# Windowed attention with 20-wide heads: 64 score products in the edge set become 32, and 16 in each main set become 24

## The chip, the core and the metric

The kernel runs on one NeuronCore of a Trainium2 chip, in one launch. The metric is the device time of one execution in microseconds (us). Its engines work side by side, each through an instruction list of its own, and wait for each other by semaphores: PE (TensorE, matrix products; its weight loads are shown apart as PEld), ACT (ScalarE), DVE (VectorE), POOL (GpSimd) and SP, which here only issues transfers (DMA). Products leave PE into PSUM, a memory of eight banks; from there ACT or DVE take them into SBUF.

## What is computed

A transformer block over a sequence of 2048 rows of 640 values, with 32 heads of 20 values and a causal window of 256 keys:

```python
mod = (silu(c) @ w_mod)                    # six vectors: sa, ca, ga, sb, cb, gb
h = layernorm(x) * (1 + ca) + sa
q, k, v = split(h @ wqkv)                  # 32 heads of 20
s = q @ k.T * 20 ** -0.5
mask = (i - j >= 0) & (i - j < 256)
o = softmax(where(mask, s, -1e9)) @ v
x = x + ga * (o @ wo)
h = layernorm(x) * (1 + cb) + sb
x = x + gb * ((sigmoid(h @ w_gate) * (h @ w_up)) @ w_down)
```

w_gate and w_up are 640x1536, w_down is 1536x640. Everything is bf16 outside PSUM.

## The kernel before

The sequence is cut into 8 chunks of 256 rows (two blocks of 128). For each chunk `a` the kernel does `ln1` (layer norm), `qkv` (three projections; Q and K are brought into the layout "head values on partitions" by transposing transfers), `attention`, `outproj` and `mlp`. Work of several chunks is under way at a time, so that PE always has dense products (128x128 weights, L684) to do between the steps of the attention.

Four heads `j` lie on partitions 0, 32, 64 and 96, so a head's product uses 20 rows of one 32-row strip of PE's array, and four heads can run in the array at once. Eight groups of four heads make 32 heads. `attention(a)` treats the groups in two halves `q` of four groups `k`. For chunks 1 to 7 each half consists of five score sets, then one burst:

- The edge set (`edge_set`, L1000) takes the corners of the band for all four groups: 64 products, each of 64 keys by 64 queries, with the array cut into strips of 32 rows and 64 columns (eight places; `tp=(32 * j, 64 * half)`). ACT turns its 2048 columns of PSUM into exponentials in the tile G (L1022).
- Four main sets (`main_set`, L1028), one for each `k`: 16 products of 128 keys, with the array cut into strips of 32 rows and all 128 columns (four places), 192, 64, 64 and 192 queries wide (`PIECES`, L1026). ACT writes the exponentials into a tile E, in eight stretches of 256 out of every 384 columns (L1048). POOL then clears what lies outside the band by four selections of 512 columns (L1057): two in place, two that read the corners from G and write them into the free ends of E.
- The burst (`burst`) multiplies the exponentials by V: 64 products for each half, four 32-column strips of the array at once, a row of ones in V giving the softmax sum. DVE transposes and divides the result (`norm`), and `close` sends it through DRAM by transfers into the layout that `outproj` needs.

PSUM has one score buffer (`p_S`, four banks), so a set's products can start only after ACT has read the set before. The other four banks (`p_M`) serve everything else. E has five buffers of 3072 columns (`NE`, `EW`), G one of 2048.

A burst is done together with a score set of the next half: with `AFTER = 1` it stands in PE's list just ahead of the second of the five sets (`with_pv`). Before the change the sets of a half come in the order edge, 0, 1, 2, 3 (`plan`), so a half's burst follows the next half's edge set.

The order of every engine is fixed. Each step is an operation (`Prog.op`) with an estimated length; the list `PLAN` names, in one sequence, the operation and its engine, and `schedule` and `emit` only walk it: they give buffers, and put a wait on each operation for what it depends on. Nothing is decided at run time, so an engine whose next instruction waits stands still. Transfers are issued by SP and by ACT (`XE`, `OUTE`); which of them, and which engine does a copy or a scaling that several could do, is also in `PLAN`. At the start ten transfers bring c, the first rows of x, half of wq and five pieces of w_mod; the five products of w_mod with silu(c) (`fnA`) give the vectors `mA`, without which the first projection can't start.

## Time and profile before

| | |
|---|---|
| time, median of 3 runs | 327.04 us (326.96 to 327.34) |
| span of the profiled execution, first to last instruction | 324.6 us |
| PE busy | 318.6 us, 5044 products recorded |
| POOL busy | 187.1 us, of it 141.2 us in the masks of L1057 |
| ACT busy | 212.5 us, of it 131.3 us in the exponentials of L1048 and L1022 |
| DVE busy | 205.6 us |

The profile of an execution gives its span; its time with what lies around the span is not recorded apart, and the median of the runs is 2.4 us above the span. PE's weight loads run beside its products. A product's record has its start as the engine saw it and an end that is modelled, about 0.2 us later, so products overlap; what a group of products costs is read from start to start, which is what the chain of waits shows. In the chain, "PE S L685" is a score set, "PE M L685" a burst, "PE M L684" dense products.

### The profile page before, as it was taken

To read this page: it belongs to the slowest core of one execution; us is meant where nothing else is said; L and a number is where in the kernel's file an instruction comes from. 1 tells how busy PE (TensorE), PEld (TensorE's weight loads), DVE (VectorE), ACT (ScalarE), POOL (GpSimd) and SP (SyncE) were. 2 spreads that over 40 slices of the span, in tenths; PEclk is the share of its full clock that TensorE was granted. 3 is DMA by queue.
4 is the path that set the end of the run, shared out by engine and by line. 5 is a ranking of instruction groups with operands and counts; after the bars stand their busy time and mean duration, and the time that the engine had idled before them with its cause. 6 is when DMAs were issued, how large, how long until landed. Compare 5 with 4: busy or idle time off the path is not lost.

```text
span 324.6 us, 11948 instructions
## 1 busy us (share of the span) xinstructions
PE 318.6 (98%) x5044; PEld 239.1 (74%) x5045; DVE 205.6 (63%) x421; ACT 212.5 (65%) x228; POOL 187.1 (58%) x326
## 2 busy tenths in 40 slices
...
PEclk9999999999999999999999999999999999999999
...
GB/s 248 370 379 182 304 182 214 208 201 313 111 107 39 152 79 99 92 98 117 57 75 60 95 26 22 103 91 95 8 58 99 46 63 63 50 55 41 63 0 42
DMA packets 73023, 38.20 MB, mean 118 GB/s; under 512 B 46602, under 2 KB 71690, under 8 KB 72970
## 3 DMA queue, kind: packets, MB, share of 16 engines
...
## 4 chain that ended last, share of the span: by engine, by line
PE 91%; DMA 3%; SPq 1%; ACT 1%; issue 1%; DVE 1%; POOL 0%; POOLq 0%; DVEq 0%; ACTq 0%
PE M L684 75%; PE S L685 9%; PE M L685 6%; DMA wd<-in_w_mod_dram 2%; DMA h2T<-x 1%; SPq L574 1%; ACT E L1022 1%; SPq L808 1%; ACT hT L825 0%; DVE hT L826 0%; POOL E L1057 0%; POOL h2T L826 0%; PE S L684 0%; DVE x L801 0%; DVE V L901 0%
## 5 line engine op out<-in xcount | busy, mean ns | idle before, releaser
L1057 POOL TENSOR_SCALAR_AFFINE_SELECT E<-E 128x512 bf16<-128x512 bf16 x224 | 141.2, 662 | 65.8 <-PE S L685 25.5
L1048 ACT ACTIVATE E<-S 128x2048 bf16<-128x2048 f32 x56 | 105.0, 1876 | 32.9 <-PE S L685 32.5
L684 PE MATMUL M<-h2T,wu 128*128 128x256 bf16 x480 | 71.2, 273 | 0.1
L684 PE MATMUL M<-h2T,wg 128*128 128x256 bf16 x480 | 66.1, 273 | 0.0
L684 PE MATMUL M<-wd,hh 128*128 128x320 bf16 (+2 forms) x396 | 56.8, 295 | 0.0
L684 PEld LDWEIGHTS M<-h2T,wg 128*128 128x128 bf16 x480 | 46.3, 98 | 6.5
L684 PEld LDWEIGHTS M<-h2T,wu 128*128 128x128 bf16 x480 | 44.1, 98 | 9.1 <-issue 0.6
L1276 ACT ACTIVATE sig<-M 128x512 f32<-128x512 f32 x48 | 28.5, 595 | 33.8 <-PE M L684 32.0
L1278 DVE SCALAR_TENSOR_TENSOR hh<-sig,M 128x512 bf16<-128x512 f32 x48 | 32.2, 678 | 28.3 <-ACT sig L1276 20.7
L684 PEld LDWEIGHTS M<-wd,hh 128*128 128x128 bf16 x396 | 37.7, 98 | 13.8
L685 PE MATMUL S<-QT,KT 20*64 20x64 bf16 (+4 forms) x1856 | 35.0, 211 | 0.1
L685 PEld LDWEIGHTS S<-QT,KT 20*128 20x128 bf16 (+1 forms) x1856 | 22.1, 98 | 17.3 <-issue 8.5
L1022 ACT ACTIVATE E<-S 128x2048 bf16<-128x2048 f32 x14 | 26.3, 1877 | 13.1 <-PE S L685 12.7
L1297 DVE TENSOR_TENSOR x<-M,x 128x320 bf16<-128x320 f32 (+2 forms) x33 | 15.7, 480 | 30.2 <-PE M L684 29.9
L1142 DVE STREAM_TRANSPOSE T<-M 128x512 f32<-128x512 f32 x32 | 21.7, 699 | 13.8 <-PE S L685 12.8
L779 DVE BATCH_NORM_STATS2 st<-x 128x6 f32<-128x320 bf16 x64 | 28.6, 476 | 0.7 <-DMA x<-in_A_x_dram 0.3
L684 PE MATMUL M<-wv,hT 128*128 128x320 bf16 x160 | 27.4, 300 | 0.0
L684 PE MATMUL M<-wq,hT 128*128 128x320 bf16 x160 | 26.6, 300 | 0.4 <-issue 0.4
L684 PE MATMUL M<-wk,hT 128*128 128x320 bf16 x160 | 26.8, 299 | 0.0
L684 PE MATMUL M<-wo,oT 128*128 128x320 bf16 x160 | 25.5, 299 | 0.3 <-ACT hT L825 0.3
L1231 DVE TENSOR_TENSOR x<-M,x 128x320 bf16<-128x320 f32 x32 | 15.3, 489 | 13.0 <-PE M L684 12.8
L685 PE MATMUL M<-E,V 128*32 128x256 bf16 (+1 forms) x960 | 22.8, 246 | 0.1
...
## 6 DMA issues: line engine op xcount, KB each, us to landing
...
```

Source lines behind the costliest of these rows:

```text
L574: return e.dma_start(dst(), src())
L684: return e.matmul(o, l, r, start=st, stop=sp, skip_group_check=True)
L685: return e.matmul(o, l, r, start=st, stop=sp, tile_position=tp, skip_group_check=True)
L779: A("dve", lambda e, g, bi=bi, j=j: e.bn_stats(v(bi * 12 + j * 6, 6), src[bi].ap[:, j * 320:(j + 1) * 320]), 0.48, reads=[src[bi].r()], wr ...
L1022: A("act", lambda e, eng: e.activation(G.ap[:], Sp.ap[:], ACT.Exp, scale=SM_SCALE), 1.876, reads=[Sp.r()], writes=[G.r()], prio=3, tag=f"e ...
L1048: A("act", lambda e, eng: e.activation(wide()[:, :, 64:320], Sp.ap[:].rearrange("p j (t c) -> p (j t) c", c=256), ACT.Exp, scale=SM_SCALE) ...
L1057: A("pool", lambda e, eng, ap=ap, inp=inp, pat=pat, base=base, cm=cm: e.affine_select(ap(), inp(), pattern=pat, compare_op=ALU.is_ge, fill ...
L1142: A("dve", lambda e, g, h=h: e.transpose(T1.ap[:, 512 * h:512 * h + 512], X[h].ap), 0.694, reads=[X[h].r()], writes=[T1.r(h)], prio=3.5, t ...
L1231: A("dve", lambda e, g, ps=ps, bi=bi, half=half: e.tensor_tensor(x1[bi].ap[:, half * 320:half * 320 + 320], ps.ap[:, 0:320], x1[bi].ap[:, ...
L1276: A("act", lambda e, g, pg=pg, sg=sg: e.activation(sg.ap[:], pg.ap[:], ACT.Tanh, scale=0.5), c_act(512), reads=[pg.r()], writes=[sg.r()], ...
L1278: A("dve", lambda e, g, pu=pu, sg=sg, f0=f0: e.scalar_tensor_tensor(out=hh.ap[:, f0:f0 + 2, :], in0=sg.ap[:].rearrange("p (a b) -> p a b", ...
L1297: A("dve", lambda e, g, ps=ps, bi=bi, c0=c0, n=n: e.tensor_tensor(x1[bi].ap[:, c0:c0 + n], ps.ap[:, 0:n], x1[bi].ap[:, c0:c0 + n], op=ALU. ...
```

## The change

Per half, chunks 1 to 7:

- The edge set is replaced by `ends_set`: only the two outer pieces of the band (block -2 for the first 64 queries, block 1 for the last 64), as 32 products of 128 keys by 64 queries, four places at once. Its exponentials go to the outer quarters of a G that is twice as wide (4096 columns), and POOL clears two triangles in it by two selections of 1024 columns.
- Each main set has 24 products of 64 keys, in three pairs of 256, 192 and 64 queries: the halves of a key block lie beside each other in the array (eight places; `PIECES`). The set then holds the two inner key blocks in full plus two corners of 64x64 that were parked in columns which the band leaves empty. ACT writes 2048 columns in one piece into E, which has 2048 columns now and six buffers. POOL does, for each of two sides, a selection of 256 columns that carries a corner from E into the inner quarters of G (`side`), and then one of 512 columns in place (`mask`).
- The burst reads blocks 0 and -1 from E and blocks -2 and 1 from G. The number and the widths of its products stay.
- The order of the sets is 0, 1, ends, 2, 3. The burst of the half before still comes ahead of the second set, which is now a main set, and follows main set 0.
- `PLAN` is new as a whole: all engines' orders, and which engine does what. Against the kernel before, ACT has 14 more operations, 8 of them transfers that SP issued; DVE 11 fewer; POOL 33 more, 28 of them masks and sides; SP 8 fewer. PE has the same 959 operations. At the start, the second piece of wq is issued ahead of w_mod and the first x rows of SP come after the first piece of w_mod; DVE does both statistics of x before the last step of silu(c), on which the w_mod products wait.

In the diff the numbers of `PLAN` are left out, and the last lines, which only hand G on.

```diff
@@ -351,118 +351,120 @@
 
 
 PLAN = [
...
 ]
 TR1 = 2
 NPH = 2
@@ -486,8 +488,8 @@
 FILL = 1
 WSE = (("dve", "pool"), ("dve", "pool"))
 QMAX = 4.5
-NE = 5
-EW = 3072
+NE = 6
+EW = 2048
 PAIR = 0
 PAIRO = 0
 XHP = ((2, 0), (3, 0), (4, 0), (4, 1), (5, 0), (5, 1))
@@ -537,9 +539,9 @@
     p_QT = sbpool("QT", 3, [128, NG, CH])
     p_KT = sbpool("KT", 4, [128, NG, CH])
     p_V = sbpool("V", 8, [128, H * VW + 10])
-    Eall = sb("E", [128, NE * EW + 2048])
+    Eall = sb("E", [128, NE * EW + 4096])
     p_E = Pool("E", [Eall[:, i * EW:(i + 1) * EW] for i in range(NE)])
-    p_G = Pool("G", [Eall[:, NE * EW:NE * EW + 2048].rearrange("p (j c) -> p j c", j=4)])
+    p_G = Pool("G", [Eall[:, NE * EW:NE * EW + 4096]])
     p_T1 = sbpool("T1", 1, [128, 1024], F32)
     p_Tn = sbpool("Tn", 1, [128, 1024])
     p_On = sbpool("On", 1, [128, 1024])
@@ -981,7 +983,7 @@
         if a == 0:
             return [([(0, 0, 0, 2, 0), (1, 0, 0, 2, 2)], ((0, 2, 2),), ()), ([(2, 0, 0, 2, 0), (3, 0, 0, 2, 2)], ((0, 2, 2),), ()),
                     ([(k, 1, 1, 1, k) for k in range(4)], ((0, 1, 4),), ())]
-        return [None, 0, 1, 2, 3]
+        return [0, 1, None, 2, 3]
 
     def with_pv(name, sc, dur, rd, tiles, before, mode):
         if before is None:
@@ -997,33 +999,42 @@
         return A("pe", both_of, pd + 0.09 + dur, reads=list(rd), writes=[tiles[-1].r(), X[0].r(), X[1].r()], prio=10, lat=0.2,
                  tag=f"pvs{pa}", extra=last["s"], mode=2, mout=mode, hold=tiles[:-1] + X)
 
-    def edge_set(a, q, before):
-        G, Sp = Tile(p_G, f"G{a}_{q}"), Tile(p_S, f"S{a}_{q}e")
-
-        def sc(e, eng):
-            ins = None
-            for k in range(4):
-                gi = 4 * q + k
-                for u in range(2):
-                    for half, kb in ((0, u), (1, u - 2)):
-                        kc, kl = (2 * a + kb) // 2, (kb % 2) * 128 + half * 64
-                        for j in range(4):
-                            ins = mm(e, Sp.ap[64 * half:64 * half + 64, j, k * 128 + u * 64:k * 128 + u * 64 + 64],
-                                     KT[kc].ap[32 * j:32 * j + DH, gi, kl:kl + 64],
-                                     QT[a].ap[32 * j:32 * j + DH, gi, u * 128 + half * 64:u * 128 + half * 64 + 64], True, True,
-                                     tp=(32 * j, 64 * half))
-            return ins
+    def keys_of(a, kb, lo, gi, j, n):
+        kc, kl = (2 * a + kb) // 2, (kb % 2) * 128 + lo
+        return KT[kc].ap[32 * j:32 * j + DH, gi, kl:kl + n]
+
+    def set_reads(a, q):
         rd = {}
         for kb in range(-2, 2):
             rd[KT[(2 * a + kb) // 2].r((kb % 2, q))] = 1
         for bi in range(2):
             rd[QT[a].r((bi, q))] = 1
-        last["s"] = [with_pv(f"edge{a}", sc, 0.36, rd, [G, Sp], before, 3)]
-        A("act", lambda e, eng: e.activation(G.ap[:], Sp.ap[:], ACT.Exp, scale=SM_SCALE), 1.876, reads=[Sp.r()], writes=[G.r()], prio=3,
-          tag=f"exp{a}")
-        return G
-
-    PIECES = ((0, 64, 192, 0), (-2, 0, 64, 192), (1, 192, 64, 256), (-1, 0, 192, 320))
+        return rd
+
+    def ends_set(a, q, G, before):
+        Sp = Tile(p_S, f"S{a}_{q}e")
+
+        def sc(e, eng):
+            ins = None
+            for k in range(4):
+                gi = 4 * q + k
+                for x, (kb, q0) in enumerate(((-2, 0), (1, 192))):
+                    for j in range(4):
+                        ins = mm(e, Sp.ap[:, j, k * 128 + x * 64:k * 128 + x * 64 + 64], keys_of(a, kb, 0, gi, j, 128),
+                                 QT[a].ap[32 * j:32 * j + DH, gi, q0:q0 + 64], True, True, tp=(32 * j, 0))
+            return ins
+        last["s"] = [with_pv(f"ends{a}", sc, 0.29, set_reads(a, q), [G, Sp], before, 1)]
+        cell = lambda: G.ap.rearrange("p (m c) -> p m c", c=256)
+        A("act", lambda e, eng: e.activation(cell().rearrange("p m (x c) -> p m x c", c=64)[:, :, 0:4:3, :],
+                                             Sp.ap[:].rearrange("p j (k x c) -> p (j k) x c", x=2, c=64), ACT.Exp, scale=SM_SCALE),
+          1.876, reads=[Sp.r()], writes=[G.r("A"), G.r("D")], prio=3, tag=f"exp{a}")
+        for key, c0, pat, base, cm in (("A", 0, [[0, 16], [-1, 64]], -1, 1), ("D", 192, [[0, 16], [1, 64]], 64, -1)):
+            A("pool", lambda e, eng, c0=c0, pat=pat, base=base, cm=cm: e.affine_select(
+                cell()[:, :, c0:c0 + 64], cell()[:, :, c0:c0 + 64], pattern=pat, compare_op=ALU.is_ge, fill=0.0, base=base,
+                channel_multiplier=cm), c_pool(1024), reads=[G.r(key)], writes=[G.r(key)], prio=5, tag=f"mask{a}", extra=last["s"])
+
+    PIECES = (((0, 0, 0, 256, 0), (-1, 64, 0, 256, 256)), ((-1, 0, 0, 192, 256), (0, 64, 64, 192, 64)),
+              ((1, 0, 128, 64, 448), (-2, 64, 64, 64, 0)))
 
     def main_set(a, q, k, G, before):
         E, Sp = Tile(p_E, f"E{a}_{q}_{k}"), Tile(p_S, f"S{a}_{q}_{k}")
@@ -1031,35 +1042,29 @@
 
         def sc(e, eng):
             ins = None
-            for kb, q0, n, c0 in PIECES:
-                kc, kl = (2 * a + kb) // 2, (kb % 2) * 128
+            for pair in PIECES:
                 for j in range(4):
-                    ins = mm(e, Sp.ap[:, j, c0:c0 + n], KT[kc].ap[32 * j:32 * j + DH, gi, kl:kl + 128],
-                             QT[a].ap[32 * j:32 * j + DH, gi, q0:q0 + n], True, True, tp=(32 * j, 0))
+                    for half, (kb, lo, q0, n, c0) in enumerate(pair):
+                        ins = mm(e, Sp.ap[64 * half:64 * half + 64, j, c0:c0 + n], keys_of(a, kb, lo, gi, j, 64),
+                                 QT[a].ap[32 * j:32 * j + DH, gi, q0:q0 + n], True, True, tp=(32 * j, 64 * half))
             return ins
-        rd = {}
-        for kb in range(-2, 2):
-            rd[KT[(2 * a + kb) // 2].r((kb % 2, q))] = 1
-        for bi in range(2):
-            rd[QT[a].r((bi, q))] = 1
-        last["s"] = [with_pv(f"score{a}", sc, 0.213 + 0.03, rd, [E, Sp], before, 1)]
-        wide = lambda: E.ap[:].rearrange("p (m c) -> p m c", c=384)
-        fine = lambda: E.ap[:].rearrange("p (j t c) -> p j t c", j=4, t=2)
-        A("act", lambda e, eng: e.activation(wide()[:, :, 64:320], Sp.ap[:].rearrange("p j (t c) -> p (j t) c", c=256), ACT.Exp, scale=SM_SCALE),
-          1.876, reads=[Sp.r()], writes=[E.r()], prio=3, tag=f"exp{a}")
-        out_r = [E.r()]
-        src = lambda: G.ap[:].rearrange("p j (k t c) -> p j k t c", k=4, t=2)[:, :, k]
-        for key, ap, inp, pat, base, cm in (
-                ("d", lambda: wide()[:, :, 64:128], lambda: wide()[:, :, 64:128], [[0, 8], [1, 64]], 64, -1),
-                ("f", lambda: wide()[:, :, 256:320], lambda: wide()[:, :, 256:320], [[0, 8], [-1, 64]], -1, 1),
-                ("hd", lambda: fine()[:, :, :, 0:64], src, [[0, 4], [0, 2], [1, 64]], 0, -1),
-                ("hf", lambda: fine()[:, :, :, 320:384], src, [[0, 4], [0, 2], [-1, 64]], -65, 1)):
-            A("pool", lambda e, eng, ap=ap, inp=inp, pat=pat, base=base, cm=cm: e.affine_select(
-                ap(), inp(), pattern=pat, compare_op=ALU.is_ge, fill=0.0, base=base, channel_multiplier=cm),
-              c_pool(512), reads=[E.r() if len(key) == 1 else G.r()], writes=[E.r(key)], prio=5, tag=f"mask{a}",
-              extra=last["s"])
-            out_r.append(E.r(key))
-        return E, out_r
+        last["s"] = [with_pv(f"score{a}", sc, 0.25, set_reads(a, q), [E, Sp], before, 3)]
+        part = lambda c0, n: E.ap.rearrange("p (j c) -> p j c", j=4)[:, :, c0:c0 + n]
+        side = lambda c0: G.ap.rearrange("p (j k c) -> p j k c", j=4, k=4)[:, :, k, c0:c0 + 64]
+        A("act", lambda e, eng: e.activation(part(0, 512), Sp.ap[:], ACT.Exp, scale=SM_SCALE), 1.876, reads=[Sp.r()],
+          writes=[E.r("C"), E.r("B")], prio=3, tag=f"exp{a}")
+        for key, hkey, c0, hc, near in (("C", ("A", k), 0, 64, True), ("B", ("D", k), 384, 128, False)):
+            far_h = near
+            src = c0 if near else c0 + 64
+            A("pool", lambda e, eng, hc=hc, src=src, far_h=far_h: e.affine_select(
+                side(hc), part(src, 64), pattern=[[0, 4], [-1 if far_h else 1, 64]], compare_op=ALU.is_ge, fill=0.0,
+                base=-65 if far_h else 0, channel_multiplier=1 if far_h else -1), c_pool(256), reads=[E.r(key)], writes=[G.r(hkey)],
+              prio=5, tag=f"side{a}", extra=last["s"])
+            A("pool", lambda e, eng, c0=c0, near=near: e.affine_select(
+                part(c0, 128), part(c0, 128), pattern=[[0, 4], [1 if near else -1, 128]], compare_op=ALU.is_ge, fill=0.0,
+                base=0 if near else -1, channel_multiplier=-1 if near else 1), c_pool(512), reads=[E.r(key)], writes=[E.r(key)],
+              prio=5, tag=f"mask{a}", extra=last["s"])
+        return E, [E.r("C"), E.r("B")]
 
     def score_set(a, q, si, ps, md, mf, before):
         E, Sp = Tile(p_E, f"E{a}_{q}_{si}"), Tile(p_S, f"S{a}_{q}_{si}")
@@ -1100,7 +1105,7 @@
                 out_r.append(E.r((kind, c0)))
         return E, out_r
 
-    def burst(a, q, sets, Es):
+    def burst(a, q, sets, Es, G):
 
         X = [Tile(p_M, f"O{a}_{q}x"), Tile(p_M, f"O{a}_{q}y")]
         X[0].mate, X[1].mate = X[1], X[0]
@@ -1109,13 +1114,14 @@
             ins = None
             seen = set()
             for (E, _), k in zip(Es, range(4)) if a else ():
-                for kb, q0, n, c0 in ((0, 0, 256, 0), (-2, 0, 128, 256), (1, 128, 128, 384), (-1, 0, 256, 512)):
+                for kb, q0, n, side, c0 in ((0, 0, 256, 0, 0), (-2, 0, 128, 1, 0), (1, 128, 128, 1, 128), (-1, 0, 256, 0, 256)):
                     bank = k // 2
                     oc = (k % 2) * 256 + q0
                     for j in range(4):
                         h = 4 * (4 * q + k) + j
+                        src = G.ap[:, (4 * j + k) * 256 + c0:(4 * j + k) * 256 + c0 + n] if side else E.ap[:, j * 512 + c0:j * 512 + c0 + n]
                         ins = mm(e, X[bank].ap[32 * j:32 * j + 32, oc:oc + n], V[2 * a + kb].ap[:, h * VW:h * VW + 32],
-                                 E.ap[:, j * 768 + c0:j * 768 + c0 + n], (bank, j) not in seen, True, tp=(0, 32 * j))
+                                 src, (bank, j) not in seen, True, tp=(0, 32 * j))
                         seen.add((bank, j))
             for (E, _), st in zip(Es, sets) if not a else ():
                 for k, kb, u, n, cu in st[0]:
@@ -1130,6 +1136,8 @@
         rd = {}
         for E, rs in Es:
             rd.update(dict.fromkeys(rs))
+        if G is not None:
+            rd.update(dict.fromkeys([G.r("A"), G.r("D")] + [G.r((x, k)) for x in "AD" for k in range(4)]))
         for kb in range(-2 if a else 0, 2):
             rd[V[2 * a + kb].r(0)] = 1
             rd[V[2 * a + kb].r(1)] = 1
@@ -1152,11 +1160,11 @@
 
     pend = []
 
-    def later(a, q, sets, Es, close):
+    def later(a, q, sets, Es, G, close):
         made = []
 
         def first():
-            made.append(burst(a, q, sets, Es))
+            made.append(burst(a, q, sets, Es, G))
             return made[0]
         return first, lambda: close(q, made[0][4])
```

7 lines of the change are left out of this document (4 added, 3 removed), and 226 rows, old and new, of the table PLAN.

## The prediction, made before the changed kernel had run

> **What bounds the kernel now.** I read the busy times of the page first, then the chain of waits by engine.
>
> ```profile
> PE 318.6 (98%) x5044; PEld 239.1 (74%) x5045; DVE 205.6 (63%) x421; ACT 212.5 (65%) x228; POOL 187.1 (58%) x326
> PEclk9999999999999999999999999999999999999999
> PE 91%; DMA 3%; SPq 1%; ACT 1%; issue 1%; DVE 1%; POOL 0%; POOLq 0%; DVEq 0%; ACTq 0%
> ```
>
> PE is busy for 98% of the span at its full clock, and the chain that ends last is 91% PE. A busy PE can still hide small waits, so the next view is PE's own waits between 11 and 324 us:
>
> ```profile
> PE M L684 <- issue: 0.4, 1, 0.4
> PE M L684 <- ACT hT L825: 0.3, 1, 0.3
> ```
>
> After the first projection at 11.21 us PE stands still for 0.7 us in all, in two places. The rest of the 324.6 us is 11 us of start and about 2.4 us of ending. So what a change takes out of PE's list leaves the time nearly one for one, as long as no other engine comes to be late, and there is almost no standing time to win. The chain for one half of chunk 6 shows what the attention costs PE:
>
> ```profile
> 205.57 0.64 PE S L685 x64
> 206.21 2.50 PE M L684 x18
> 208.71 1.43 PE M L685 x64
> 210.14 0.34 PE S L685 x16
> 210.48 2.51 PE M L684 x22
> 212.99 0.34 PE S L685 x16
> 225.84 1.43 PE M L685 x64
> ```
>
> The edge set holds PE for 0.64 us, a main set for 0.34, a burst for 1.43. There are 14 halves in chunks 1 to 7: 14 edge sets are 9.0 us and 56 main sets 19.0 us. Only these can shrink; the burst has the same products after the change, and so have the dense parts.
>
> **Price of the new ends set.** Cutting one edge set and one main set off at later and later times (products in order of time; start, then time to the modelled end of the last one) shows their inner course:
>
> ```profile
> 102.12 0.23 PE L685 MATMUL S<-QT,KT 20*64 20x64 bf16 x8
> 102.12 0.27 PE L685 MATMUL S<-QT,KT 20*64 20x64 bf16 x16
> 102.12 0.33 PE L685 MATMUL S<-QT,KT 20*64 20x64 bf16 x32
> 102.12 0.71 PE L685 MATMUL S<-QT,KT 20*64 20x64 bf16 x64
> ...
> 112.34 0.29 PE L685 MATMUL S<-QT,KT 20*128 20x192 bf16 x8
> 112.34 0.32 PE L685 MATMUL S<-QT,KT 20*128 20x192 bf16 x12
> 112.34 0.40 PE L685 MATMUL S<-QT,KT 20*128 20x192 bf16 x16
> ```
>
> The first 32 products of an edge set end after 0.33 us, eight more every 0.03 us; the other 32 take 0.38 us, 12 ns each, though they have the same shape and the same eight places. Something supplies the first 32 at once and the rest one by one. In the main set four products of 64 columns take 0.03 us (x8 to x12). The new ends set has 32 products, eight rounds of four: the first round's 0.23 and seven of 0.03 make 0.44, against 0.71, so it saves 0.27 us. Were its products supplied at 12 ns each, it would be 0.20 + 32 x 0.012 = 0.58 and save 0.13; were it as cheap as the whole main set (0.40), 0.31. I take 0.27, since 32 is just the number that went fast here: 14 x 0.27 = 3.8 us saved, bounds 1.8 and 4.3.
>
> [...]
>
> **Price of the new main sets.** Each place in the array now takes 256 + 192 + 64 = 512 query columns, as each of the four took 192 + 64 + 64 + 192 = 512 before. 24 products are under 32, so none should come late. What is added is that eight places fill one after the other instead of four: the edge set's x8 row is 0.23 where one of its products has 0.20 (202 ns mean, below), so some 0.02 us more. Below: nothing. Above: a round of eight 64-column products takes (0.33 - 0.23) / 3 = 0.033 us against 0.03 for four; if that tenth goes with the columns, it costs 0.02 on a main set's 0.21 us of columns, so 0.04 with the filling, and 0.06 is my upper end with rounding. I take 0.02: 56 x 0.02 = 1.1 us lost, bounds 0 and 3.4.
>
> ```profile
> L685 PE MATMUL S<-QT,KT 20*128 20x192 bf16 x448 | 22.5, 247 | 0.1
> L685 PE MATMUL S<-QT,KT 20*128 20x64 bf16 x448 | 12.7, 188 | 0.0
> L685 PE MATMUL S<-QT,KT 20*64 20x64 bf16 x896 | 10.1, 202 | 0.0
> ```
>
> The count of score products stays: 448 + 448 + 896 = 1792 = 14 x 32 + 56 x 24.
>
> **Other engines.** ACT's exponentials keep 2048 columns, and their layout has not mattered:
>
> ```profile
> L1048 ACT ACTIVATE E<-S 128x2048 bf16<-128x2048 f32 x56 | 105.0, 1876 | 32.9 <-PE S L685 32.5
> L1022 ACT ACTIVATE E<-S 128x2048 bf16<-128x2048 f32 x14 | 26.3, 1877 | 13.1 <-PE S L685 12.7
> L1057 POOL TENSOR_SCALAR_AFFINE_SELECT E<-E 128x512 bf16<-128x512 bf16 x224 | 141.2, 662 | 65.8 <-PE S L685 25.5
> L1094 POOL TENSOR_SCALAR_AFFINE_SELECT E<-E 128x1024 bf16<-128x1024 bf16 x4 | 4.4, 1096 | 2.7 <-ACT E L1086 2.7
> 219.19 6.21 POOL L1057 TENSOR_SCALAR_AFFINE_SELECT E<-E 128x512 bf16<-128x512 bf16 x10 [0.71 <-PE S L685]
> ```
>
> Gapped writes (L1048) and contiguous ones (L1022) both take 1.88. POOL: 16 selections of 0.662 are 10.6 us per half before. After: a column costs (1096 - 662) / 512 = 0.85 ns, so 256 columns take 0.445; eight of these, eight of 0.662 and two of 1.096 are 11.05 us, 6.4 us more over the kernel. It costs PE nothing while POOL keeps up: POOL has some 17 us per half (208.71 to 225.84). Before, its last ten masks run from 219.19 to 225.40 and the burst starts at 225.84: 0.4 us to spare. In the new list the half's last main set stands, counted in products at these prices, at least 6.1 us ahead of the burst; after its products (0.40) and its exponential (1.88) 3.8 us are left for 2.2 us of sides and masks. So cover shrinks in POOL's sum but not at its end. The extra wait is in G: it has one buffer, so the sides of main set 0 wait for the burst of the half before, and POOL's masks behind them; the burst waits for POOL in turn one half later.
>
> The score buffer: a set must wait for the exponential of the one before. The tightest stretches of the new list have 18 dense products of 256 columns between two sets, as here, where no wait shows:
>
> ```profile
> 78.85 0.34 PE S L685 x16
> 79.19 2.07 PE M L684 x18
> 81.26 0.33 PE S L685 x16
> ```
>
> There they follow an ends set or a main set, whose last product ends 0.02 us later: nothing to 0.3 us in all. ACT's eight transfer issues from SP (0.4 us each, estimated from SP's 2.38 for five below) and the moved scalings are covered by ACT's 35% idle; without that they would delay an exponential and with it the next set.
>
> **The start.** The last piece of w_mod sets when projections begin:
>
> ```profile
> GB/s 248 370 379 182 304 182 214 208 201 313 111 107 39 152 79 99 92 98 117 57 75 60 95 26 22 103 91 95 8 58 99 46 63 63 50 55 41 63 0 42
> 0.79 0.44 SPq L574 DMA_DIRECT2D wq<-in_A_wqkv_dram  x1
> 1.30 0.47 SPq L574 DMA_DIRECT2D x<-in_A_x_dram  x1
> 1.81 2.38 SPq L574 DMA_DIRECT2D wd<-in_w_mod_dram  x5
> 3.70 6.12 DMA wd<-in_w_mod_dram
> 11.21 6.25 PE M L684 x59
> ```
>
> It lands at 9.82 us with the transfers at 370 GB/s. In the new list a further 160 KB piece of wq goes ahead of it: 160 KB / 370 GB/s = 0.43 us later, and an issue of 0.48 us more, in the same time. If the transfers have slack early on (248 GB/s in the first slice), nothing. I take 0.3. The x rows that come later put the last step of silu(c) behind both statistics on DVE, so the first w_mod products start a us or so later; they then run one after the other until the last piece is there, which ends later anyway.
>
> **The sum**, against the profiled execution: -3.8 + 1.1 + 0.3 = -2.4 us, standing time unchanged. The span goes from 324.6 to 322.2; the 2.4 us from the span to the median stay: 327.04 - 2.4 = 324.6 us.
>
> **The rivals.** (a) *The halves do not stream beside each other for nothing*: main sets at the upper bound, 0.06 each. For it: no row has eight places with 256 columns. Against: the rounds of eight above. -3.8 + 3.4 + 0.3 = -0.1: 326.9 us, no change. (b) *POOL comes late at the burst* (the slower end): through the single G, POOL has 11.05 us of masks to do between one burst and the next, beside its other work, and each burst waits for the last of them. It decides from 0.17 us per half on (2.4 / 14). For it: 0.4 us to spare before, and 0.45 us more work per half; against it: the last main set stands earlier. At 0.4 us per half: 324.6 + 5.6 = 330.2 us. (c) *Second halves wait for first halves*: `main_set` now issues both halves of a head in turn, in one 32-row strip. If a weight load had to wait for the strip's running product, a set would take four heads x 512 columns one after another; 22 products of 256 columns take 2.51 us, 0.114 each, so 0.91 us and not 0.23, and 56 x 0.68 makes 38 us: about 363 us. Against it: in the edge set products 5 to 8 sit in the strips of products 1 to 4, and the eight end within 0.23 us, when one alone takes 0.20. [...] (d) *All goes as well as it can*: ends sets save 4.3, main sets cost nothing, the start 0.1: 322.8 us.
>
> **How the numbers follow.** The forecast has 0.60, (a) 0.10, (b) 0.14, (c) 0.02, (d) 0.14. About 0.2% (0.65 us) is what a measurement tells from no change. Forecast and (d) are faster, 0.74; (a) is the same, 0.10; (b) and (c) are slower, 0.16. The likeliest case alone spans 323.6 to 325.8. The range from 322.8, case (d), to 327.2, just beyond (a), leaves out (b) and (c), 0.16.
>
> **What would show it.** Right: in the chain the ends sets stand at about 0.36 us, the main sets at 0.36, bursts still at 1.43; the first projection at about 11.5; PE's waits from there under 1 us. Wrong: bursts that wait for POOL, sets that wait for ACT's exponentials, a chain with more than a few us off PE behind the start, main sets of 0.4 us and more, or a first projection after 12 us.

## The result, and the profile after

The changed kernel is slower: 330.01 us median (327.09 to 333.52, 20 runs) against 327.56 us (326.03 to 329.77, 20 runs) of the kernel before on the same chip, a ratio of 1.006 with an interval of 1.0032 to 1.0089. (The ratio and its interval, here and below, leave out runs that are over 1.5% above the fastest of their kernel, five of the changed kernel's 20; the medians leave out none.) The forecast was 324.6 us, and its range ended at 327.2. The profiled run took 327.98 us, with a span of 326.1 us against 324.6 before.

The busy line and the chain by engine of the changed kernel, from its page:

```profile
PE 316.4 (97%) x5044; PEld 236.9 (73%) x5045; DVE 203.4 (62%) x410; ACT 214.7 (66%) x234; POOL 193.7 (59%) x359
...
PE 86%; DMA 4%; POOL 3%; DVE 2%; ACT 2%; issue 1%; SPq 1%; POOLq 0%; DVEq 0%; ACTq 0%
```

PE works 2.2 us less than before (316.4 against 318.6), yet the span is 1.5 us longer: PE stands still for longer. The share of the chain that is not PE went from 9% to 14%.

**The score sets came out as priced.** The chain of one stretch of the changed kernel (start, length, engine, line, products):

```profile
209.90 1.43 PE M L687 x64
211.34 0.36 PE S L687 x24
211.69 2.29 PE M L686 x20
213.98 0.34 PE S L687 x32
```

An ends set holds PE for 0.34 us where the edge set took 0.64, a main set for 0.36 instead of 0.34, a burst for 1.43 as before. Over all sets, from the start of a set's first product to the start of the product behind it, the medians are 0.345 against 0.639 and 0.359 against 0.335: 14 x -0.294 + 56 x 0.024 = -4.1 + 1.3 = -2.8 us.

**The start.** SP's and PE's timelines of the changed kernel (start, length, engine and line, operation; in brackets the idle time before it and what ended that), and behind them the step of its chain that ends the wait for w_mod:

```profile
0.79 0.97 SPq L576 DMA_DIRECT2D wq<-in_A_wqkv_dram  x2
1.81 0.48 SPq L576 DMA_DIRECT2D wd<-in_w_mod_dram  x1
2.33 0.43 SPq L576 DMA_DIRECT2D x<-in_A_x_dram  x1
2.80 1.86 SPq L576 DMA_DIRECT2D wd<-in_w_mod_dram  x4
...
7.95 0.74 PE L686 MATMUL S<-silubc,wd 128*128 128x64 bf16 x20 [1.44 <-ACT silubc L657]
...
12.56 1.53 PE L686 MATMUL M<-wq,hT 128*128 128x320 bf16 x10 [0.71 <-DVE hT L820]
```

```profile
4.23 6.90 DMA wd<-in_w_mod_dram
```

The last piece of w_mod leaves 0.53 us later than before (4.23 against 3.70) and is under way for 0.78 longer (6.90 against 6.12). It lands at 11.13 instead of 9.82, and the first projection starts at 12.56 instead of 11.21: 1.35 us later.

**What PE waits for behind the start** (14 to 324 us; us in total, times, longest):

```profile
PE M L686 <- ACT h2T L827: 1.3, 1, 1.3
PE M L687 <- issue: 0.6, 1, 0.6
PE M L686 <- DVE grow L736: 0.5, 1, 0.5
PE M L686 <- DVE st L781: 0.4, 1, 0.4
PE M L687 <- POOL E L1063: 0.3, 1, 0.3
PE S L687 <- issue: 0.3, 1, 0.3
```

That is 3.4 us where the kernel before had 0.3, in one place. (Of the two rows that the prediction adds to 0.7, the first, 0.4, ends where the first projection starts, as this line of the kernel before shows, and so belongs to the start.)

```profile
11.21 2.06 PE L684 MATMUL M<-wq,hT 128*128 128x320 bf16 x14 [0.45 <-issue]
```

All six waits lie between 26 and 110 us; behind that the changed kernel wins some 0.2 us with each half. Start +1.35, sets -2.8, standing time +3.1: the sum is +1.65, and the two spans differ by 1.5.

The largest waits lead back to transfers. Below are two stretches of SP's list in the changed kernel, from 12 to 23 us and around 68 us, the first with the product that waited for it; and then the chain behind the second:

```profile
12.37 2.14 SPq L576 DMA_DIRECT2D wu<-in_w_mod_dram  x4
21.22 0.81 SPq L576 DMA_DIRECT2D x<-in_A_x_dram  x2
22.07 0.43 SPq L576 DMA_DIRECT2D wu<-in_w_mod_dram  x1
...
26.17 0.88 PE L687 MATMUL M<-wu,silubc 128*32 128x160 bf16 x40 [0.64 <-issue]
...
66.17 1.58 SPq L810 DMA_TRANSPOSE KT<-stg  x1
68.46 2.53 SPq L810 DMA_TRANSPOSE h2T<-x  x2
```

```profile
69.71 4.60 DMA h2T<-x
...
74.84 0.60 ACT h2T L827
...
75.57 1.50 PE M L686 x11
```

The fifth piece of w_mod's second part ("wu"; tag wm1) is issued at 22.07: in SP's new list it comes behind two loads of x that wait until 21.22, and SP can't pass them. The kernel before issued all five pieces in one go, by 14.7 us. The 40 products that need it then stand at 26.17. At 68.46 SP issues the two transposing transfers that turn the second layer norm of chunk 0 (h2T); before, it did so at 64.83. They come at the end of a row of transposing transfers, each of which holds SP for 1.2 us or more, and the second takes 4.60 us to land.

That row is not new. From the first Q transfer in it to the second h2T SP issues eleven transposing transfers in both kernels, and two loads of w_down among them. In the kernel before this takes 19.2 us (46.87 to 66.10), of which SP waits for 1.7; in the changed kernel 23.3 us (46.40 to 69.71), of which it waits for 4.3, before transfers of oT, K and hT. The other 1.4 us are issues, as three more transfers stand in the row ("gate", "oT" and "wg").

### The profile page after: what moved, and what is told of

Its sections match the earlier page's. It is cut to its first block, busy times and chain, and to the rows that moved or that the text cites. A ratio compares the mean times of both kernels' runs of the same rounds, so it can differ in the third digit from the quotient of the medians.

```text
span 326.1 us, 11997 instructions
## 1 busy us (share of the span) xinstructions
PE 316.4 (97%) x5044; PEld 236.9 (73%) x5045; DVE 203.4 (62%) x410; ACT 214.7 (66%) x234; POOL 193.7 (59%) x359
## 4 chain that ended last, share of the span: by engine, by line
PE 86%; DMA 4%; POOL 3%; DVE 2%; ACT 2%; issue 1%; SPq 1%; POOLq 0%; DVEq 0%; ACTq 0%
PE M L686 72%; PE S L687 7%; PE M L687 7%; DMA wd<-in_w_mod_dram 2%; DMA h2T<-x 1%; POOL E L1063 1%; ACT E L1054 1%; SPq L576 1%; POOL E L1032 1%; POOL E L1059 1%; ACT E L1028 1%; DVE st L781 1%; DVE T L1150 0%; ACT hT L827 0%; DVE Tn L1157 0%
## 5 line engine op out<-in xcount | busy, mean ns | idle before, releaser
L1059 POOL TENSOR_SCALAR_AFFINE_SELECT E<-E 128x256 bf16<-128x256 bf16 x112 | 45.6, 421 | 49.8 <-PE S L687 14.3
L1063 POOL TENSOR_SCALAR_AFFINE_SELECT E<-E 128x512 bf16<-128x512 bf16 x112 | 69.9, 639 | 5.1 <-DVE Tn L1157 1.3
L686 PE MATMUL M<-h2T,wu 128*128 128x256 bf16 x480 | 67.4, 273 | 1.3 <-ACT h2T L827 1.3
L686 PE MATMUL M<-h2T,wg 128*128 128x256 bf16 x480 | 65.3, 273 | 0.0
L686 PEld LDWEIGHTS M<-h2T,wu 128*128 128x128 bf16 x480 | 45.0, 98 | 9.2 <-issue 1.4
L1032 POOL TENSOR_SCALAR_AFFINE_SELECT E<-E 128x1024 bf16<-128x1024 bf16 x28 | 31.8, 1145 | 7.6 <-PE M L686 3.4
L687 PE MATMUL S<-QT,KT 20*64 20x256 bf16 (+5 forms) x1856 | 32.3, 228 | 0.3 <-issue 0.3
L687 PEld LDWEIGHTS S<-QT,KT 20*64 20x64 bf16 (+1 forms) x1856 | 20.0, 101 | 17.1 <-issue 7.9
L686 PE MATMUL M<-wk,hT 128*128 128x320 bf16 x160 | 27.9, 300 | 0.0
L686 PE MATMUL M<-wo,oT 128*128 128x320 bf16 x160 | 24.7, 299 | 0.4 <-DVE st L781 0.4
```

Source lines behind the costliest of these rows:

```text
L686: return e.matmul(o, l, r, start=st, stop=sp, skip_group_check=True)
L687: return e.matmul(o, l, r, start=st, stop=sp, tile_position=tp, skip_group_check=True)
L1032: A("pool", lambda e, eng, c0=c0, pat=pat, base=base, cm=cm: e.affine_select(cell()[:, :, c0:c0 + 64], cell()[:, :, c0:c0 + 64], pattern=p ...
L1059: A("pool", lambda e, eng, hc=hc, src=src, far_h=far_h: e.affine_select(side(hc), part(src, 64), pattern=[[0, 4], [-1 if far_h else 1, 64] ...
L1063: A("pool", lambda e, eng, c0=c0, near=near: e.affine_select(part(c0, 128), part(c0, 128), pattern=[[0, 4], [1 if near else -1, 128]], com ...
```

## The experiments

A number of `PLAN` is 5 x step + engine (PE 0, ACT 1, DVE 2, POOL 3, SP 4). The diffs show the order of one engine's steps as `PLAN` gives it. "The stand at 74" and the like is the delay of a product from start to start.

### Is it the start, or w_mod's stuck piece?

**e1_wm1** puts the stuck piece ahead of the loads of x that wait.

```diff
 SP: wm1 179, wm1 184, wm1 174, wm1 164,
-    x6 1534, x7 1539, wm1 169, wm2 194
+    wm1 169, x6 1534, x7 1539, wm2 194
```

> Changed kernel, with the fifth piece of w_mod's second tile issued ahead of the two x loads that wait on SP (in the changed kernel it was issued at 22.07 us, behind a load that stood from 14.5 to 21.2). Theory Q (a transfer stuck behind a waiting one holds up the second w_mod product): PE's standing of 0.8 us before that product at 26.2 us goes, and what follows moves up by 0.6 to 0.8 us; ratio to the kernel before about 0.002 lower than the changed kernel's 1.006. Theory T (the new list is tight everywhere in the first 76 us, so a wait removed comes back at the next place): the 0.8 us goes there and is stood again before 76 us; time as the changed kernel's.

**e2_start** puts the transfers and the last step of silu(c) at the start back as they stood in the kernel before.

```diff
 SP:
-    wq 129, wq 124, wm0 99, x0 89, wm0 104, wm0 109, wm0 114, wm0 119, wq 134
+    wq 124, x0 89, wm0 99, wm0 104, wm0 109, wm0 114, wm0 119, wq 129, wq 134
 DVE:
-    372, 367, 377 (statistics of x1), 207 (c_col), 357, 352, 362 (of x0), 217 (siluc)
+    207 (c_col), 217 (siluc), 372, 367, 377, 357, 352, 362
 PE:
-    warm 240, ctr 200
+    ctr 200, warm 240
```

> Changed kernel with its first 12 us put back: wq's second piece behind the five w_mod pieces, the first x rows ahead of them, the transpose of c two warming products earlier, and the steps of silu(c) on DVE and ACT ahead of the statistics of x. Theory Q: the first projection moves from 12.56 us to about 11.3 and everything behind it by 1.2 us; ratio about 0.004 lower than the changed kernel's. Theory T: the start is won, and later standing grows by as much, since the transfers of weights do not come earlier; time within 0.3 us of the changed kernel's.

**e3_both** makes both edits.

> Both edits together. Theory Q, with the later standing (44.9, 52.2, 61.1, 75.6 us, 3.1 us in all) as a consequence of the late start: 4 us off the changed kernel, ratio about 0.994 to the kernel before. Theory Q for these two places alone: 2 us off, ratio about 1.000. Theory T: no more than 0.5 us off.

**e4_ends64** leaves the changed kernel's order alone and cuts each of an ends set's 32 products into two of 64 keys: 64 products for the same values.

```diff
-                        ins = mm(e, Sp.ap[:, j, k * 128 + x * 64:k * 128 + x * 64 + 64], keys_of(a, kb, 0, gi, j, 128),
-                                 QT[a].ap[32 * j:32 * j + DH, gi, q0:q0 + 64], True, True, tp=(32 * j, 0))
+                        ins = mm(e, Sp.ap[64 * half:64 * half + 64, j, k * 128 + x * 64:k * 128 + x * 64 + 64],
+                                 keys_of(a, kb, 64 * half, gi, j, 64),
+                                 QT[a].ap[32 * j:32 * j + DH, gi, q0:q0 + 64], True, True, tp=(32 * j, 64 * half))
```

> Changed kernel with each of the 32 products of an ends set cut into two of 64 keys, 64 products in eight places as the old edge set had; nothing else changes. If the products beyond the 32nd are supplied one by one, the ends set goes back from 0.34 to about 0.64 us in the chain: 14 x 0.29 = 4.1 us slower than the changed kernel, as far as PE sets the time after 76 us (12 sets, 3.5 us). If the cost is in the shape and not in the number, or if PE does not set the time, less than 1 us slower.

Measured, beside 326.66 us of the kernel before (23 runs):

| | median us | ratio to before | first projection | stands of PE over 0.3 us behind it |
|---|---|---|---|---|
| e1_wm1 | 330.28 | 1.0103 [1.0056, 1.0149] | 13.81 | 1.13 at 47, 1.14 at 54, 1.55 at 69, 0.39 at 78, 0.39 at 112 |
| e2_start | 328.91 | 1.0065 [1.0035, 1.0095] | 11.35 | 0.81 at 51, 2.26 at 67, 0.39 at 111 |
| e3_both | 327.88 | 1.0019 [0.9993, 1.0046] | 10.98 | 0.50 at 50, 0.48 at 59, 1.99 at 74, 0.39 at 110 |
| e4_ends64 | 334.63 | 1.0228 [1.0177, 1.028] | 12.08 | 1.50 at 43, 1.94 at 68, 0.39 at 112 |

The edits do where they were made what they should: the stand at 26 us is gone in e1, the first projection is early in e2 and e3. But e1 is no faster for it, and e2 hardly: both come out near theory T. In e1's profiled run PE waits 2.43 us for silu(c) in the start, which e1 leaves as it was, and has half its clock from 7.94 to 11.36 us; none of its six runs kept the full clock. And e3, near theory Q for these two places alone, with both causes mended and its score sets 2.8 us cheaper, only reaches the kernel before. Its largest stand ends like that of the changed kernel, in h2T. Then comes something more: three stretches of e3_both, one with most of the stand, one behind it and one later (us; busy times with instructions; granted clock; DMA share; GB/s):

```profile
71.60:73.60 2.00, 0.52 (x32) 0.27 (x24) 0.79 (x3) 0.79 (x2) 0.00 (x0) 1.00 1.00 284
75.10:78.40 3.30, 3.30 (x47) 2.18 (x44) 2.92 (x7) 1.37 (x2) 1.96 (x4) 0.50 1.07 384
79.00:82.00 3.00, 3.00 (x48) 2.33 (x47) 0.69 (x1) 2.66 (x3) 1.47 (x2) 1.00 0.09 30
```

From 75.1 us at the latest, 1.1 us after the stand of 1.99 us, PE has half its clock, for 3.3 us at least: half of that, some 1.7 us, is lost on top of the stand. e4 settles the price of an ends set. Its chain has

```profile
217.91 0.64 PE S L687 x64
```

where 32 products took 0.34. What the products compute is the same; their number and their shape (64 keys, eight places) are those of the edge set again. That it is the number follows from the course of the set: cut off behind the 32nd product, e4's set, too, has ended after 0.33 us, with the same shape. 14 x 0.30 is 4.2 us, and e4 is 4.6 us slower than the changed kernel by the medians, 5.5 by the ratios.

### What did the start alone cost?

**e7_before_start** is the kernel before with the first 68 entries of the changed kernel's `PLAN` at its head and the rest of its own behind them. On SP this is the order that e2_start undid, the other way round:

```diff
 SP:
-    wq 124, x0 89, wm0 99, wm0 104, wm0 109, wm0 114, wm0 119, wq 134, wq 129
+    wq 129, wq 124, wm0 99, x0 89, wm0 104, wm0 109, wm0 114, wm0 119, wq 134
```

> The kernel before, with only the first steps of all engines in the order of the changed kernel (a piece of wq ahead of w_mod, x later, the last step of silu(c) behind the statistics of x); score sets, masks and everything from the first projection on as before. Theory (the start alone costs the changed kernel 1.35 us, and little of it is won back): first projection at 12.3 to 12.8 us instead of 11.2, time 0.9 to 1.5 us above the kernel before. Rival 1 (the prediction's 0.3 us): first projection at 11.5, time +0.1 to +0.4. Rival 2 (a late start throws this list out of step too, as it holds its transfers as tightly): +2 us and more, with new stands of PE.

Measured: 328.90 us (327.20 to 330.22, 10 runs) against 327.46, ratio 1.0042 [1.0018, 1.0067]: the start alone costs 1.4 us, which is in the theory's range. But little of it is the late projection as such. In the profiled run the first projection starts at 13.54, later than expected. The reason shows in PE's wait for silu(c), from the timeline, and in the clock behind it, from the table of stretches (the column behind POOL's is the granted clock):

```profile
8.12 1.12 PE L684 MATMUL S<-silubc,wd 128*128 128x64 bf16 x18 [2.65 <-ACT silubc L655]
```

```profile
8.00:11.00 3.00, 2.88 (x38) 2.37 (x39) 0.45 (x1) 0.00 (x0) 1.14 (x3) 0.53 1.06 369
```

Here PE waited 2.65 us for the last step of silu(c), and was at half clock afterwards. Six of the ten runs had such a stretch, and their median is 329.7 us; the four without have 327.6, next to the kernel before. Of the 29 runs of the kernel before beside them, three had one.

**e8_silu** keeps the transfers of the changed start, and has only silu(c) early and the stuck piece mended.

```diff
 DVE:
-    372, 367, 377 (statistics of x1), 207 (c_col), 357, 352, 362 (of x0), 217 (siluc)
+    207 (c_col), 217 (siluc), 372, 367, 377, 357, 352, 362
 PE:
-    warm 240, ctr 200
+    ctr 200, warm 240
 SP: wm1 164,
-    x6 1534, x7 1539, wm1 169
+    wm1 169, x6 1534, x7 1539
```

> The kernel of e3_both with the transfers of the start as in the changed kernel (wq's second piece ahead of w_mod, x behind the first piece of w_mod); only the last step of silu(c) stays ahead of the statistics of x, and w_mod's fifth piece ahead of the loads that wait. It tells apart which half of the start's change cost. Theory (the transfers: the last piece of w_mod lands at 11.1): first projection at 12.2 us or later, as in the changed kernel (12.56). Rival (silu(c) behind the statistics of x kept the first product of w_mod waiting): first projection at 11.0 to 11.4, as in e3_both (10.98).

Measured: first projection at 12.71 us (one run, 329.99 us). In this run the clock was full there, so the transfers alone make the projection late, though silu(c) was early. The order of silu(c) cost more than the wait itself where half clock came with it: with waits of 2.65 us in e7 and 2.43 in e1.

### Can the waits between 40 and 78 us be moved away?

All four start from e3_both.

**e5_h2t** moves the two h2T transfers forward in SP's list.

```diff
 SP: qkt3 2539, qkt3 2574, wd 1984,
-    qkt3 2609, qkt3 2644, gin 1219, btr0 1949, btr0 1944, wg0 329
+    btr0 1944, qkt3 2609, btr0 1949, qkt3 2644, gin 1219, wg0 329
```

> The kernel of e3_both, and in SP's list the two transfers that bring the layer norm of chunk 0 into the layout for the MLP (h2T<-x) are taken from behind the last two transfers of Q and K of chunk 3: the first stands ahead of both, the second between them. Theory (what still stands between 50 and 76 us is SP's list: each transposing transfer holds SP for 1.25 us, and h2T came at its end): the two h2T are issued at about 62.6 and 65.3 us instead of 66.66 and 67.9, the second lands by 70.5 instead of 72.8, PE's stand of 1.99 us at 74 us falls under 0.6, no stretch at half clock follows it, and the time is 324.5 to 326.0 us, below the kernel before. Rival 1 (SP's list is not what h2T waits for): the stand stays at 1.7 us or more and the time within 0.5 of e3_both's 327.9. Rival 2 (the loss only moves): this stand goes, but others of 1 us and more in all come up elsewhere, time 326.5 to 327.5.

Measured: 329.01 us (327.75 to 332.43, 10 runs), ratio 1.0052 [1.0021, 1.0083]. The second h2T is issued at 66.25, the stand at 74 is gone, and a stand of 2.00 us appears at 65.75 instead, with a stretch at half clock behind it. That is rival 2 in kind; the time is 1.5 us above what it gave. The place shows how one late transfer reaches PE, in ACT's timeline (idle time before, in brackets):

```profile
63.34 0.60 ACT L827 ACTIVATE hT<-hT,mA 128x256 bf16<-128x256 bf16 x1 [2.20 <-DMA hT<-x]
63.84 1.85 ACT L1054 ACTIVATE E<-S 128x2048 bf16<-128x2048 f32 x1
```

ACT waits 2.2 us for the transposing transfer of chunk 4 (hT); the exponential of a score set that has been ready since 61.7 stands behind it, and PE's next set needs the score buffer.

**e6_all** mends each stand of e3_both in the list of the engine that seemed to cause it: h2T and its input earlier, Q of chunk 2 behind the read of the attention output, two steps of POOL into a hole.

```diff
 DVE:
+    bxh0 1937 (from behind amodu4 2797 to here)
     evqk3 2602
 SP:
+    btr0 1944, btr0 1949 (from behind gin 1219 to here)
     qkt3 2609
 SP: oT_0 1729,
-    qkt2 1364, gout 1214, oT_0 1829
+    gout 1214, oT_0 1829, qkt2 1364
 POOL: mask2 4278,
+    side2 4243, mask2 4248 (from behind side2 4383 to here)
```

> The kernel of e3_both with four steps moved, each against one of PE's remaining stands: both h2T transfers of chunk 0 ahead of the last two of chunk 3's Q and K, and DVE's normalisation that feeds the second one 0.5 to 1 us of list earlier (stand of 1.99 us at 74); a transfer of Q of chunk 2 behind the read of the first half's attention output instead of ahead of it (stand of 0.50 at 50 us); one side and one mask of POOL into a hole of its list at 98 us (burst late by 0.39 at 110 us). Theory: these three stands fall by 2.0 us or more in all and PE keeps its full clock; time 324.0 to 325.5 us, below both kernels. Rival (the order holds no slack, so that each step put earlier makes another late): other stands take their place, time 326.5 to 328.

Measured: 329.97 us (327.11 to 331.97, 12 runs), ratio 1.0046 [1.0013, 1.008]. That is the rival in kind; the time is 2 us above what it gave. The profiled run has the longest stand yet, from the chain:

```profile
48.15 3.62 DMA QT<-stg
51.77 0.14 issue
51.91 1.11 PE M L686 x5
```

Q of chunk 2, which I had put one place back, is now what a projection's buffer waits for: 2.58 us, and half clock again.

**e9_act** is e5_h2t with ACT's scaling that waited put behind the exponential, and the two steps of POOL from e6_all.

```diff
 ACT:
-    amodu4 2786, exp1 3086
+    exp1 3086, amodu4 2786
```

> The kernel of e5_h2t, with two steps more: in ACT's list the first scaling of hT of chunk 4, which waits for a transposing transfer, goes behind the exponential that stood behind it (in the profile of e5_h2t ACT waits 2.2 us for that transfer from 61.1 on, the exponential of a set that has been ready since 61.68 starts at 63.84, and the next score set stands 2.00 us at 65.75), and POOL's side and mask of e6_all go into the hole at 98 us. Theory (a stand of PE arises where one late transfer holds an engine's list and a ready exponential queues behind it): the stand of 2.00 us and the half clock behind it go, what is left by the late hT is under 0.7 us at the next projections, the burst at 110 us is not late (0.39 saved); time 1.5 to 3.5 us below e5_h2t, that is 0.9945 to 1.0005 of the kernel before. Rival (PE has nothing else to do there: the projections that come next need hT too): the stand moves to the projections with 1.5 us or more, time as e5_h2t, 1.003 to 1.007.

**e10_wu** is e9_act with one load of w_up earlier.

```diff
 SP: n_ow_0 1719,
+    wu0 1159
     atr3 1604, atr3 1599,
-    wu0 1159,
     n_ow_0 1809
```

> The kernel of e9_act, and the load of the second half of w_up (576 KB) is issued at about 36.5 us, ahead of the transposing transfers of chunk 3, instead of 39.4, 2.8 us ahead of the writes of the attention output that the output projection needs back. Theory (that load keeps those writes waiting: issued by 43.7, the read behind them goes out only at 47.65, 1.2 us later than in the kernel before): the read goes out by 46.8, the stand of 0.99 us at 50.5 (e5_h2t) falls under 0.4; time 0.4 to 1.0 us below e9_act. Rival (the transfers' total is what limits, not their order): the chunk 3 transposes land later by as much, a stand of 0.5 us or more appears between 38 and 48 us, time that of e9_act or above.

Measured: e9_act 330.35 us (327.61 to 333.48, 10 runs), ratio 1.0071 [1.0036, 1.0105]; e10_wu 329.67 us (326.82 to 330.81, 10 runs), ratio 1.006 [1.0028, 1.0092]. The stand at 65.75 is gone in e9, as the theory had it for that one place, but PE stands 1.55 us at 44, 0.86 at 52 and three times 0.59 between 66 and 72. In e10 the read of the attention output costs 0.52 instead of 0.99 us (e5_h2t), but products with h2T stand three times for 0.9 us at 76 to 78, with half clock behind them. In time e9 and e10 can't be told apart. From the first projection to the end the kernel before takes 313.4 us, e5 315.2 and e9 314.8. A single step put earlier makes another one late: up to here the waits were only moved.

### Are the transposing transfers the cause?

**e11_plain_before**, **e12_plain_after** and **e13_plain_e3** are the kernel before, the changed one and e3_both, with plain copies in place of all transposing transfers. (There are 52 of them; the expectation counts 44.)

```diff
-            return e.dma_start_transpose(dst(), src())
+            return e.dma_start(dst(), src().rearrange("p (t c) -> p t c", c=128))
```

> The kernel before, with all 44 transposing transfers (hT, h2T, QT, KT) made plain copies of the same bytes into the same places, so that values arrive untransposed: the transposition is left out and the output is not the reference's, all products, exponentials, masks and waits stay. It is the control for the next two. A plain issue should hold SP for about 0.4 us instead of 1.25 and land in some 2 us instead of 3 to 5. PE's waits after the first projection were 1.2 us in all before, so at most that is to be won: time 0.5 to 1.5 us below the kernel before; with other stands none.

> The changed kernel with the same plain copies; transposition left out as in the control. Theory (after the start, what PE waits for in the changed kernel are the transposing transfers, each of which holds SP and lands late): of the 4.5 us of PE's waits between 26 and 110 us at most 1.7 are left (0.8 of them the stuck piece of w_mod at 26), and the kernel is 0.3 to 1.5 us faster than the control: the score sets' 2.8 less the start's 1.4 and that piece. Rival (the order of DVE, ACT and POOL makes PE wait, whatever the transfers do): 3 us or more of waits stay, 1 to 2.5 us slower than the control.

> The kernel of e3_both (start and stuck piece of w_mod mended) with the same plain copies; transposition left out as in the control. Theory: PE's waits from 24 to 110 us fall under 1.2 us, no stretch at half clock, and the kernel is 2.0 to 3.2 us faster than the control, which is what the score sets give. Rival: 2.5 us of waits or more stay, within 1 us of the control.

Measured, beside 326.91 us of the kernel before (20 runs):

| | median us | ratio to before | runs at full clock throughout |
|---|---|---|---|
| e11_plain_before | 326.72 | 0.9989 [0.996, 1.0017] | 9 of 10 |
| e12_plain_after | 326.64 | 0.9984 [0.9953, 1.0015] | 4 of 10 |
| e13_plain_e3 | 324.30 | 0.9912 [0.9878, 0.9946] | 5 of 5 |

PE's waits from 12 us on, in e13_plain_e3 and then in e12_plain_after:

```profile
PE M L686 <- ACT h2T L827: 1.2, 1, 1.2
PE M L687 <- POOL E L1099: 0.4, 1, 0.4
PE M L687 <- POOL E L1063: 0.3, 1, 0.3
```

```profile
PE M L686 <- DVE hT L820: 0.7, 1, 0.7
PE S L687 <- issue: 0.6, 1, 0.6
PE M L687 <- POOL E L1099: 0.4, 1, 0.4
PE M L687 <- POOL E L1063: 0.3, 1, 0.3
```

(The first row of e12 is the wait for the first projection at 14.05.) With plain copies e13 is 2.4 us faster than its control, near the 2.8 us of the score sets. By the ratios the kernel before gains 0.1% from them, the changed one 0.8% (1.006 to 0.9984, 2.5 us), e3_both 1.1% (1.0019 to 0.9912, 3.5 us). So most of what the changed kernel lost is gone once the start is mended and no transfer transposes; in the kernel before the same transfers cost nothing that can be told from noise. Not all waits go: h2T is still waited for, 1.2 us, and the 1.9 us in all that e13 shows are above the expected 1.2. e11 misses its expectation of 0.5 to 1.5 us, as there was next to nothing to win. e12 misses its own by a little: its start is late, six of its ten runs fall to half clock, and its four runs at full clock have a median of 324.89 us, 1.3 us below the control's 326.17.

A transposing transfer differs first in what it takes from SP. The median issue is 1.25 us, of a plain copy 0.60; all 52 together hold SP for 72.8 us in the changed kernel, 35.6 in e13. To the landing no steady difference shows: the medians in the kernel before and in its control are 4.7 and 3.5 us for h2T, 2.7 and 2.6 for hT, 3.0 and 3.0 for Q, so not the 2 us that the expectation gave a plain copy. In e13 the second h2T takes

```profile
66.02 5.46 DMA h2T<-x
```

against 4.60 in the changed kernel and 4.87 in e3_both; in the control, though, the first h2T landed 3.49 us after its issue began, in the kernel before 5.48.

### Is it SP's list?

**e14_wd** starts from e3_both, keeps the transposing transfers and takes two loads of w_down (480 KB each) out from between them; DVE's scalings of w_down go behind.

```diff
 SP:
-    wd 1979 (behind qkt2 1399), wd 1984 (behind qkt3 2574)
+    wd 1984 (behind wd 1994), wd 1979 (behind n_ow_1 3049)
 DVE:
-    wds 2012, 2017, 2022 (around bmodu0 1962), wds 1997 (ahead of wds 2012)
+    wds 2012, 2017, 2022 (behind glu_0 2172), wds 1997 (ahead of wds 2002)
 POOL: as in e6_all
```

> The kernel of e3_both, all transposing transfers kept, and three things moved: the two loads of w_down (480 KB each), which SP issued between 53 and 62 us among the transposing transfers of chunks 2 to 4, go behind the h2T transfers of chunk 0 (69 us and later); DVE's four scalings of w_down that wait for them go behind with them (the first product that needs them comes after 90 us); POOL's side and mask go into the hole at 98 us. Theory (the transposing transfers are late because SP's list and the queue hold more between 45 and 70 us than fits): h2T goes out 1 us earlier, the waits of 40 to 78 us fall from 3.0 us and a stretch at half clock to under 1.5 us with none, the burst at 110 us is not late; time 324.5 to 326.0 us, faster than both kernels. Rival 1 (it is the landing time of the transposing transfers themselves, 4 to 5.5 us, that the order doesn't allow for): waits of 2.5 us or more stay, time 327 to 328.5. Rival 2: the loads now come late for the writes and reads of the attention output of chunk 1, with new waits between 78 and 100 us.

**e15_wd_h2t** adds the moves of e5_h2t and e9_act.

> The kernel of e14_wd, with the h2T transfers of chunk 0 ahead of the last two of chunk 3's Q and K (as in e5_h2t) and ACT's first scaling of hT of chunk 4 behind the exponential (as in e9_act). Theory: no wait of PE over 0.6 us between 40 and 78 us, time 324.0 to 325.5 us. Rival (order shifts only where the same lateness shows): waits of 2 us and more in all, time 327 to 329.

Measured beside 327.11 us: e14_wd 331.91 us (330.99 to 335.57, 6 runs), ratio 1.0165 [1.0125, 1.0204]; e15_wd_h2t 335.59 us (332.19 to 336.75, 6 runs), ratio 1.0238 [1.0196, 1.0281]. Both missed. PE's waits in e14_wd:

```profile
PE M L687 <- POOL E L1063: 4.0, 1, 4.0
...
PE M L686 <- ACT h2T L827: 0.4, 1, 0.4
```

The wait for h2T fell from 1.9 to 0.4 us, but a burst came 4 us late: DVE's scalings stood behind the first products of the gate, and POOL, with masks to do, stood 5.86 us until they were done. It is the late burst of the prediction's rival (b), but brought about by a scaling on another engine. In e15 a burst is 4.05 us late in the same way, products with h2T stand 2.99 us at 78.5, and half clock follows each of the two.

**e16_wd2** puts three of those scalings into a hole of DVE's list instead.

```diff
 DVE: astats5 3367, astats5 3362,
+    wds 2012, wds 2017, wds 2022,
     glu_0 2112, ..., glu_0 2172
-    wds 2012, wds 2017, wds 2022
```

> The kernel of e14_wd, but DVE's three scalings of the second load of w_down stand in a hole of DVE's list (78 to 81 us in the profile of e3_both) instead of behind the first products of the gate, where they held POOL's masks up until the burst at 92 us came 4.1 us late. Theory (the transposing transfers are late because SP and the queue hold the loads of w_down between them): as e14_wd up to 78 us, where the stand at 74 us fell from 1.99 to 0.48 us, no burst late by over 0.3 us, no stretch at half clock behind 60 us; time 324.8 to 326.3 us, below the kernel before. Rival (the landing time itself): waits of 2.5 us and more between 40 and 78 us, time 327 to 328.5.

**e17_act** is e16_wd2 without the two moved steps of POOL and with ACT's order of e9_act; **e18_h2t_act** has the two h2T of e5_h2t moved as well.

> The kernel of e16_wd2 without the two steps of POOL at 98 us (in its profile they only moved the wait: no late burst, but 0.73 us at 103 us, behind POOL's statistics), and with ACT's first scaling of hT of chunk 4 behind the exponential, as in e9_act. Theory: of e16_wd2's waits 0.76 at 64.6 us and 0.73 at 103 us go, 0.39 at the burst comes back: time 325.5 to 326.3 us, below the kernel before. Rival (the lateness of hT only shows elsewhere): 326.7 to 327.5, as e16_wd2.

> The kernel of e17_act, with the two h2T transfers of chunk 0 ahead of the last two of chunk 3's Q and K, as in e5_h2t. Theory: the remaining 0.65 us of wait at 73.5 us goes too, time 325.0 to 326.0 us. Rival: Q and K of chunk 3 or hT of chunk 4 are late in their place, time 326.7 us or more.

Measured:

| | median us | lowest to highest, runs | ratio to before |
|---|---|---|---|
| e16_wd2 | 326.96 | 325.37 to 331.52, 12 | 0.9989 [0.9966, 1.0012] |
| e17_act | 325.35 | 324.87 to 330.08, 12 | 0.9953 [0.9928, 0.9978] |
| e18_h2t_act | 328.64 | 326.02 to 331.90, 12 | 1.0029 [0.9995, 1.0063] |

e16 missed its expected 324.8 to 326.3 by 0.7 us. The waits of PE from 14 us on in it

```profile
PE S L687 <- ACT E L1054: 0.7, 1, 0.7
PE M L686 <- ACT h2T L827: 0.6, 1, 0.6
PE M L686 <- DVE x L1306: 0.6, 1, 0.6
PE M L687 <- POOL E L1099: 0.4, 1, 0.4
PE M L686 <- ACT hT L827: 0.3, 1, 0.3
```

sum to 2.6 us; the third of them, at 103 us, lies by the chain behind POOL's statistics, which its moved steps had put back. In e17 neither the first nor the third is there. It is faster than the kernel before by 0.47% (1.5 us) and so beats both kernels. Eleven of its twelve runs kept the full clock, ten lie between 324.87 and 326.50; the profiled one, 328.28, is an outlier with a wait of 1.9 us for "grow", the gate from w_mod, at 45 us. e18 shows that this list, too, is full: with the two h2T earlier, products with h2T stand 3.15 us at 78 us (for what, the profile doesn't show), six of the twelve runs have a stretch at half clock, and 3.3 us are lost against e17.

So the wait for h2T falls from 1.9 us to 0.4 (e14) or 0.6 (e16, e17) when the loads are out of the row: they were a part of what made it late. In time, only the loads and ACT's order together (e17) are clear of e3_both; e16 alone is not. What is left between e17 and the plain copies of e13 (0.9953 against 0.9912, 1.3 us) can't be divided by these runs between SP's hold and the landing; that stays open.

## Why the prediction was wrong

- **Ends set, 0.27 us saved: right**, 0.30 by the chain, 0.294 by starts. That 32 products come at once and the next 32 one by one is confirmed by e4, with 0.33 us to the end of the 32nd product and 0.64 us for the set of 64.
- **Main set, 0.02 us lost: right** (0.024). Rival (a), 0.06, and rival (c), 0.68, fall with it.
- **Start, 0.3 us with an upper end of 0.43: mis-sized.** The first projection comes 1.35 us later in the profile. (The 1.4 us in time of e7 are for the most part half clock.) I counted the further 160 KB piece of wq as 0.43 us of transfer and its issue of 0.48 as lying in the same time. They add up: the last piece left 0.53 us later and took 0.78 longer.
- **silu(c) behind both statistics, "which ends later anyway": right at full clock** (e8 gains nothing by it), but it rested on PE's wait being without consequence. In e7 that wait was 2.65 us, and half clock came after it.
- **"Standing time unchanged": the step that failed.** It grew by 3.1 us in the profile and turned a gain of 1.5 us into a loss of 1.5. I had priced ACT's, POOL's and DVE's moved work, and each queue's first issues, but not walked SP's new list against the times at which its transfers can be issued. Two things in that list could have been read before the run: a piece of w_mod behind two loads that wait, and three more transfers in the row of transposing ones between 46 and 71 us. The hold of the transposing transfers was there before; what the change adds is that SP waits 2.6 us longer in the row, so that the second h2T goes out 3.6 us later. With plain copies and a mended start the kernel gains 2.4 us on its control (e13); with the loads of w_down out of the row and ACT's order changed as well, 1.5 us on the kernel before (e17). How the 3.1 us divide between SP's hold, its waits, the landing and the other engines' orders stays open.
- **Clock: not in the prediction.** Its row of the kernel before was full from end to end, so I took a wait to cost what it lasts. But a stretch at half clock came with or behind single waits of 1.99 us (e3) and 2.65 us (e7) and, in e10, 2.2 us of waits within 3.42 us (see the last section): a loss of up to 1.7 us more. By their mean granted clock 14 of the 20 runs of the changed kernel had at least one such stretch; the six without have a median of 327.95 us. So about 0.4 of the 2.45 us between the medians is lost at full clock, where a gain of 2.4 had been forecast, and the rest in runs with half clock.
- **Rival (b), POOL late at the burst**, was right in its mechanism and wrong in its reach: one burst, at 110 us, came 0.39 us late, not each of 14.
- **Two readings were off and change nothing.** The 0.7 us of standing time before were 0.3, as said above. And the 2.4 us between span and time are 1.7 to 2.1 in every run that lists both; the forecast went by differences.
